# Reading the attention terms in natural query order on TensorE (moving operand with a stride of 32 words), with unstrided evictions on ScalarE

## The chip, the cores and the metric

The kernel runs on one core of a Trainium2 chip. A core has five engines that work side by side: TensorE (PE, matrix products, with a separate row PEld for loading its weights), VectorE (DVE), ScalarE (ACT), GpSimd (POOL) and SyncE (SP), which here issues all the transfers (DMAs). TensorE reads its operands from SBUF, the on-chip memory of 128 partitions, and writes its results to PSUM, from where ScalarE or VectorE fetch them ("evict" them) to SBUF. The metric is the device time of one execution in microseconds, as a median of several runs.

## The reference

There are 8 batches of 12 heads, 448 positions and 64 values per head. Attention with a soft cap comes first, and its result, with the heads side by side, goes through a gated block:

```
scores = cap * tanh(q @ k.T / 8 / cap)
attn   = exp(scores - max(scores))
attn   = attn / (sum(attn) + 1e-9)
x      = attn @ v                          # heads joined: 448 x 768
h      = relu(x @ w_in);  u, v = halves of h (512 each)
v_n    = (v - mean(v)) / sqrt(var(v) + 1e-6)
v_s    = w_spatial @ v_n + b_spatial
out    = (u * v_s) @ w_out
```

## The kernel before

The kernel has two bodies and a branch on the cap; with the cap of 30 the one for small caps runs (`pair_bnd`), in which no maximum has to be subtracted ahead of the exponential. Work on the attention goes by pairs of heads: 6 pairs in each of 8 batches, 48 in all. After the six pairs of a batch come the gated block's matrix products for that batch (`moe`), which are mixed on TensorE with the next batch's pairs.

The host hands over q with its 448 positions reordered. Position 14 i + b (i from 0 to 31, b from 0 to 13) stands in column 32 b + i. Everything up to the second product is in this order, "b outside, i inside", because VectorE's transposition of 32x32 blocks in the reduction needs the 32 positions of a block side by side.

The steps of one pair, with the names that the profile shows:

- One DMA brings q and k (`raw`). ScalarE makes the rounded copy `qh`, VectorE the remainder `ql`.
- TensorE forms the scores (L540) into `ps_s`, in two halves `j` of two blocks of 112 keys each, for both heads: keys on the partitions, queries along the free axis.
- ScalarE takes the tanh (L545) out of PSUM into `tp`, and then the exponential (L550) in place. `tp` is 112 partitions by 4 x 448 numbers: two key blocks by two heads. These are the terms of the softmax. There are two such tiles per pair.
- TensorE multiplies the terms with v (L559) into `ps_x`: the first head's result goes to PSUM partitions 0 to 63, the second's to 64 to 127. Four matmuls for each half, eight for a pair, accumulated over the four key blocks. There is one buffer of `ps_x`.
- ScalarE evicts `ps_x` to `xf` (L564). This copy also brings the positions back to natural order: it reads PSUM in order and writes SBUF with a stride of 14 words.
- The sums of the terms: for the first 10 pairs (`PE_SUMS`) TensorE forms them too, with a matrix of ones (L599) into a `ps_acc` buffer, eight matmuls into four groups of 32 PSUM partitions. ScalarE evicts them to `sx` (L602), again with the stride of 14 words. Four small DMAs bring four rows of `sx` to memory (`td`) and two more bring them back to `dt` with the positions across partitions. For the other 38 pairs VectorE does the sums, as it does the maxima for all of them (`red`, L580 to L587, then `st`, `md`, `dt`).
- VectorE forms the reciprocals in `dt`, DMAs bring them out (`rd`) and back, broadcast over the partitions (`rr`). GpSimd multiplies `xf` by `rr` (L645), and the result, split into a rounded part and a remainder (`xg`), is what the gated block reads.

The order of the work is made when the kernel is built. `Plan` simulates the engines with a duration for each task, and always starts the task with the lowest key among those whose inputs and buffers are there. The order that comes out is each engine's program. The durations are estimates written into the code: `act(S)` is 0.833 x 448 + 51 = 424 ns; the eviction of the second products has `act(S)`, that of the sums has 951 ns. TensorE's tasks of the second products and of the sums count 2 x 760 ns each.

Of the kernel before, what the change touches and what calls it, by code (L numbers as in the profile page):

```python
# [16 lines left out]
B, H, S, D = 8, 12, 448, 64  # L17
# [4 lines left out]
QB = 14  # L22
# [20 lines left out]
class Plan:  # L43
# [14 lines left out]
    def add(self, eng, dur, key, fn, deps=(), uses=(), allocs=(), lat=0.0, name="", mode="N"):  # L58
        t = Task()
        t.eng, t.dur, t.key, t.fn, t.lat, t.name, t.mode = eng, float(dur), key, fn, lat, name, mode  # L60
        t.lock = eng == "P" or eng == "V" and name not in self.OWN
        t.deps = [d for d in deps if d is not None]
        t.allocs = list(allocs)
        t.uses = list(dict.fromkeys(list(uses) + t.allocs))
        for u in t.uses:
            u.users += 1
        t.seq = len(self.tasks)
        self.tasks.append(t)
        return t
# [103 lines left out]
def act(n, extra=0):  # L173

    return 0.833 * n + 51 + 93 * extra


def act_s(n, extra=0):

    return 0.833 * n + 94 + 93 * extra  # L180
# [14 lines left out]
def gpc(n):  # L195
# [6 lines left out]
KB = S // 4  # L202
# [23 lines left out]
               ev=3.19, x=2.62, moe=0.79, span=12.63, step=0.24, mv=-1.51)  # L226
# [13 lines left out]
def attn_moe(ctx, tc, bounded, shared, qk, v, qk2, v2, cap, w_in, w_sp, w_out, out):  # L240
    nc = tc.nc
# [45 lines left out]
    if bounded:  # L287
# [4 lines left out]
        one = const.tile([128, 32], F32, name="one")  # L292
# [9 lines left out]
    add = plan.add  # L302
# [216 lines left out]
    def pair_bnd(b, hp, xf, rr):  # L519
# [3 lines left out]
        kk = lambda name, n=0: at + KEY[name] + KEY["step"] * n  # L523
# [7 lines left out]
        x, tps, exps, prev = Buf("x"), [], [], None  # L531
        for j in range(2):
            ps, tp = [Buf("s"), Buf("s")], Buf("tp")

            def scores(j=j, ps=ps):
                for i in range(2):
                    for n, (y, z) in enumerate(((qh, qh), (ql, qh), (qh, ql))):
                        for e in range(2):
                            r, c = slice(e * D, (e + 1) * D), S + (2 * j + i) * KB
                            nc.tensor.matmul(ps[i].t[:KB, e, :S], lhsT=y.t[r, c:c + KB], rhs=z.t[r, :S], start=(n == 0), stop=(n == 2))  # L540

            s = add("T", 6 * MM, kk("sc", j), scores, [t0, t2], [qh, ql, *ps], ps, name="sc", mode="R")
            for i in range(2):
                th = add("A", act(PW, 1), kk("th", j),
                         lambda i=i, ps=ps, tp=tp: nc.scalar.activation(  # L545
                             out=tp.t[:KB, i * PW:(i + 1) * PW].rearrange("p (e q) -> p e q", q=S), in_=ps[i].t[:KB, :, :S],
                             func=AF.Tanh, scale=ic[:KB]),
                         [s], [ps[i], tp], [tp] if i == 0 else [], name="tanh")
            ex = add("A", act_s(2 * PW, 1), kk("ex", j),
                     lambda tp=tp: nc.scalar.activation(out=tp.t[:KB], in_=tp.t[:KB], func=AF.Exp, scale=ca[:KB]), [th], [tp],  # L550
                     name="exp")
            tps.append(tp)
            exps.append(ex)

            def pv(j=j, tp=tp):
                for i in range(2):
                    for e in range(2):
                        c, o = 2 * j + i, (2 * i + e) * S
                        nc.tensor.matmul(x.t[e * D:(e + 1) * D, 0, :S], lhsT=vt.t[:KB, (2 * c + e) * D:(2 * c + e + 1) * D],  # L559
                                         rhs=tp.t[:KB, o:o + S], start=(c == 0), stop=(c == 3))  # L560

            prev = add("T", 2 * FF, kk("pv", j), pv, [ex, prev, t1], [vt, tp, x], [x] if j == 0 else [], name="pv", mode="C")

        z = add("A", act(S), kk("ev"), lambda: nc.scalar.copy(  # L564
            out=xf.t.rearrange("p (i b) -> p b i", b=QB), in_=x.t[:, 0, :S].rearrange("p (b i) -> p b i", i=32)), [prev], [x, xf],
            [xf], name="xev")

# [8 lines left out]
        for a, op, engs, key in ((0, ALU.max, E_RED, "mx"), (1, ALU.add, E_SUM, "sm"))[:1 if by_pe else 2]:  # L578
# [9 lines left out]
                out=st.t[:, 2 * a * QB:2 * (a + 1) * QB], in_=blk(r.t[:, PW:]), axis=AX.X), [d, *done], [r, st],  # L588
                [st] if a == 0 else [], name="red3"))
        row = lambda y: y.rearrange("(e p c) -> p e c", e=2, c=QB)  # L590
        sums = None
        if by_pe:
            acc, sx, td = Buf("acc"), Buf("sx"), Buf("td")

            def ones():
                for c in range(4):
                    for e in range(2):
                        o, i = e * D + c % 2 * 32, (c % 2 * 2 + e) * S
                        nc.tensor.matmul(acc.t[o:o + 32, 0, :S], lhsT=one[:KB], rhs=tps[c // 2].t[:KB, i:i + S], start=(c < 2), stop=(c > 1))  # L599

            sums = add("T", 2 * FF, kk("pv", 1) + 0.01, ones, exps, [u, w, acc], [acc], name="ones", mode="Q")
            sums = add("A", 951, kk("ev"), lambda: nc.scalar.copy(  # L602
                out=sx.t.rearrange("p (i b) -> p b i", b=QB), in_=acc.t[:, 0, :S].rearrange("p (b i) -> p b i", i=32)), [sums], [acc, sx],
                [sx], name="sev")
            sums = [add("S", HW, kk("dn"), lambda r=r: nc.sync.dma_start(out=td.t[r * S:(r + 1) * S], in_=sx.t[32 * r:32 * r + 1]), [sums],
                        [sx, td], [td] if r == 0 else [], lat=XL) for r in range(4)]
            two = lambda: dt.t[:32, 8 * QB:12 * QB].rearrange("p (e g c) -> p e g c", e=2, c=QB)
            sums = [add("S", HW, kk("dn"), lambda g=g: nc.sync.dma_start(
                out=two()[:, :, g], in_=td.t.rearrange("(e g p c) -> g p e c", e=2, g=2, c=QB)[g]), sums, [td, dt], [dt] if g == 0 else [],
                lat=XL) for g in range(2)]  # L610
# [6 lines left out]
            out=sec(0), in_=grp()[:, :, :2 * QB].rearrange("p g b -> p b g"), axis=AX.X), [d], [dt], name="mred2")  # L617
# [3 lines left out]
        else:  # L621
            d1 = add("V", 185, kk("dn"), lambda: nc.vector.reduce_sum(
                out=sec(1), in_=grp()[:, :, 2 * QB:].rearrange("p g b -> p b g"), axis=AX.X), [d0], [dt], name="sred2")
# [4 lines left out]
            out=row(rd.t), in_=sec(0).rearrange("p (e c) -> p e c", c=QB)), [d], [dt], [rd], lat=XL)  # L628
        out = [add("S", HH, kk("dn"), lambda e=e: nc.sync.dma_start(
            out=rr.t[e * D:(e + 1) * D], in_=rd.t[e * S:(e + 1) * S].unsqueeze(0).broadcast_to([D, S])), [d], [rd, rr],  # L630
            [rr] if e == 0 else [], lat=XF * D * S) for e in range(2)]
        return out + [z]

    def pair(b, hp):
        k = float(b * H + 2 * hp)
        xf, rr = Buf("xf"), Buf("rr")
        if bounded:
            deps = pair_bnd(b, hp, xf, rr)
        else:
            vt, vdep = v_any(b, hp, k - 1.2)  # L640
            after = []
            deps = [d for e in range(2) for d in head_any(b, 2 * hp + e, vt, vdep, xf, rr, after)]
        g = Buf("xg")
        k += KEY["x"] if bounded else 1.3
        m = add(E_X[0], st2(E_X[0], 448), k, lambda: eng[E_X[0]].tensor_tensor(xf.t, xf.t, rr.t, op=ALU.mult), deps, [xf, rr], name="xmul")  # L645
        c = add(E_X[1], ct(E_X[1], 448), k, lambda: copy(E_X[1], g.t[:, XH:], xf.t), [m], [xf], [g], name="xh")
        d = add(E_X[2], st2(E_X[2], 448), k, lambda: sub(E_X[2], g.t[:, :S], xf.t, f(g.t[:, XH:])), [c], [xf, g], name="xl")
        t = add(E_X[3], ct(E_X[3], D), k, lambda: copy(E_X[3], g.t[:, S:XH], xf.t[:, S - D:]), [m, c], [xf, g], name="xt")
        return g, [t, d]
# [222 lines left out]
```

## Time and profile before

| | |
|---|---|
| median of 3 runs | 802.78 us (802.62 to 805.45) |
| the profiled execution | 804.6 us |
| its span, first to last instruction | 802.7 us |
| mean granted TensorE clock | 0.99 |
| TensorE matmul records of the second products (L559) | 768, 157.2 us busy |
| TensorE matmul records of the sums (L599) | 160, 17.1 us busy |
| ScalarE copies of second products (L564) | 48, 46.2 us busy |
| ScalarE copies of sums (L602) | 10, 9.8 us busy |

The profile is one execution, taken by the hardware profiler. "Busy" is the time in which at least one instruction of a group ran on its engine. Matmuls overlap: a record's own duration includes the time in which it only finishes while the next is under way, so the busy time of a group is far below the count times the mean. A matmul on numbers of full precision leaves two records. The view of waits names for each idle stretch of an engine what ended it. The chain is the work that ended last, followed back from the end of the run.

### The profile page before, as it was taken

Reading aid. Unit: us, or ns where it says so; the run is one execution under the profiler, and the core shown is the slowest. Engines: PE = TensorE matmul, PEld = TensorE weight load, DVE = VectorE, ACT = ScalarE, POOL = GpSimd, SP = SyncE. Lnnn points to the kernel's source line nnn. Section 1 sums busy time; section 2 is a strip of 40 time slices with the busy share of each in tenths; the row PEclk is TensorE's granted clock in tenths of the full one; section 3 lists DMA queues with packets and bytes.
Section 4 is the critical chain, followed back from the end, with each engine's and each line's share of the span. In section 5 each row is a group of like instructions: output and inputs, shape, how many; then the busy total and the mean of one; then the engine's idle time right before and its main releaser. Section 6 shows DMA issues by size and latency. Waiting matters only on the chain.

```text
span 802.7 us, 11490 instructions
## 1 busy us (share of the span) xinstructions
PE 763.1 (95%) x4126; PEld 528.4 (66%) x4126; DVE 707.3 (88%) x934; ACT 575.5 (72%) x699; POOL 228.6 (28%) x179
## 2 busy tenths in 40 slices
PE   6878899979999999999999999999999999999997
PEld 2333456646776766667667677767677766767796
DVE  4979997899899997999999999999999999999340
ACT  4999877595777867687678876887677876874131
POOL 3131133341242103440143313330244212431150
PEclk8999999999999999999999999999999999999999
DMA  5544532433222332124221332223221332112102
GB/s 176 182 109 125 152 111 62 125 89 121 60 61 74 97 112 58 48 62 131 75 61 50 120 97 61 69 68 113 93 59 51 107 99 68 54 52 73 38 1 73
DMA packets 51254, 69.04 MB, mean 86 GB/s; under 512 B 23754, under 2 KB 36596, under 8 KB 51188
## 3 DMA queue, kind: packets, MB, share of 16 engines
q1 hardware_dynamic: 51188, 68.22, 28.7%
q8 instruction: 34, 0.56, 0.3%
q14 instruction: 32, 0.26, 0.1%
HBM read 55.70 MB, written 12.49 MB: 85 GB/s over the span
## 4 chain that ended last, share of the span: by engine, by line
PE 54%; DVE 24%; DMA 8%; ACT 7%; issue 5%; POOL 1%; SPq 1%; ACTq 0%; DVEq 0%; POOLq 0%
PE ps_x L559 10%; DVE red L580 10%; PE ps_s L540 9%; PE ps_acc L678 4%; PE ps_acc L679 4%; PE ps_acc L680 4%; DVE red L585 3%; DVE st L587 3%; ACT tp L545 2%; DMA dt<-md 2%; PE ps_acc L772 2%; ACT tp L550 2%; PE ps_acc L774 2%; PE ps_acc L773 2%; PE ps_acc L794 2%
## 5 line engine op out<-in xcount | busy, mean ns | idle before, releaser
L545 ACT ACTIVATE tp<-ps_s,capt 112x896 f32<-112x896 f32 x192 | 184.6, 1005 | 9.9 <-PE ps_s L540 8.9
L580 DVE TENSOR_TENSOR red<-tp 112x1792 f32<-112x1792 f32 x86 | 180.6, 2110 | 10.0 <-ACT tp L550 10.0
L550 ACT ACTIVATE tp<-tp,capt 112x1792 f32<-112x1792 f32 x96 | 172.4, 1796 | 2.3
L645 POOL TENSOR_TENSOR xf<-xf,rr 128x448 f32<-128x448 f32 x48 | 86.2, 1797 | 280.1 <-DMA rr<-rd 267.6
L559 PE MATMUL ps_x<-tp,v 112*64 112x448 f32 x768 | 157.2, 549 | 4.6 <-ACT tp L550 2.7
L559 PEld LDWEIGHTS ps_x<-tp,v 112*64 112x64 f32 x768 | 50.4, 137 | 87.2 <-issue 75.7
L580 DVE TENSOR_TENSOR red<-red 112x896 f32<-112x896 f32 x86 | 103.4, 1203 | 0.5
L585 DVE STREAM_TRANSPOSE red<-red 128x896 f32<-128x896 f32 x86 | 94.0, 1093 | 0.9
L587 DVE TENSOR_REDUCE st<-red 128x28 f32<-128x896 f32 x86 | 90.8, 1077 | 1.1
L540 PE MATMUL ps_s<-qh 64*112 64x448 f32 x384 | 81.2, 417 | 10.2 <-ACT tp L545 6.4
L540 PE MATMUL ps_s<-qh,ql 64*112 64x448 f32 x384 | 72.8, 372 | 6.6 <-DVE ql L306 6.5
L306 POOL TENSOR_TENSOR xg<-o,xg 128x448 fp32r<-128x448 f32 x32 | 46.1, 1443 | 107.4 <-ACT xg L310 107.4
L540 PEld LDWEIGHTS ps_s<-qh 64*112 64x112 f32 x384 | 34.0, 173 | 63.8 <-issue 28.1
L540 PE MATMUL ps_s<-ql,qh 64*112 64x448 f32 x384 | 72.2, 368 | 0.0
L678 PE MATMUL ps_acc<-xg,wi_h 128*128 128x448 f32 x186 | 69.7, 375 | 1.3 <-ACT xg L310 1.2
L794 PE MATMUL ps_acc<-xg,wo_h 128*128 128x448 f32 x184 | 69.3, 376 | 1.5 <-DVE o L779 1.2
L679 PE MATMUL ps_acc<-xg,wi_h 128*128 128x448 f32 x186 | 68.9, 371 | 1.1 <-DVE xg L306 1.1
L795 PE MATMUL ps_acc<-xg,wo_h 128*128 128x448 f32 x184 | 67.4, 366 | 1.6 <-POOL xg L306 1.6
L680 PE MATMUL ps_acc<-xg,wi_l 128*128 128x448 f32 x186 | 68.6, 369 | 0.0
L796 PE MATMUL ps_acc<-xg,wo_l 128*128 128x448 f32 x184 | 67.4, 366 | 0.0
L310 ACT CAST xg<-xf 128x448 fp32r<-128x448 f32 x96 | 36.5, 402 | 34.3 <-POOL xf L645 31.7
L306 DVE TENSOR_TENSOR ql<-raw,qh 128x896 fp32r<-128x896 f32 x48 | 53.3, 1111 | 7.2 <-ACT qh L310 7.2
(123 smaller groups left out, 1386.7 us busy)
## 6 DMA issues: line engine op xcount, KB each, us to landing
raw<-in_qk SPq DMA_DIRECT2D x48, 448.0 KB
v<-in_v SPq DMA_DIRECT2D x48, 224.0 KB
rr<-rd SPq DMA_DIRECT2D x96, 112.0 KB
out<-o SPq DMA_DIRECT2D x48, 224.0 KB
w<-in_w_in SPq DMA_DIRECT2D x12, 512.0 KB
xg<-in_w_out SPq DMA_DIRECT2D x12, 256.0 KB
md<-st SPq DMA_DIRECT2D x38, 28.0 KB
dt<-md SPq DMA_DIRECT2D x38, 28.0 KB
```

What stands on the lines that cost most here:

```text
L306: eng[e].tensor_tensor(o, a, b, op=ALU.subtract)
L540: nc.tensor.matmul(ps[i].t[:KB, e, :S], lhsT=y.t[r, c:c + KB], rhs=z.t[r, :S], start=(n == 0), stop=(n == 2))
L545: lambda i=i, ps=ps, tp=tp: nc.scalar.activation(out=tp.t[:KB, i * PW:(i + 1) * PW].rearrange("p (e q) -> p e q", q=S), in_=ps[i].t[:KB, : ...
L550: lambda tp=tp: nc.scalar.activation(out=tp.t[:KB], in_=tp.t[:KB], func=AF.Exp, scale=ca[:KB]), [th], [tp],
L559: nc.tensor.matmul(x.t[e * D:(e + 1) * D, 0, :S], lhsT=vt.t[:KB, (2 * c + e) * D:(2 * c + e + 1) * D], rhs=tp.t[:KB, o:o + S], start=(c == ...
L580: tt = lambda g, o_, i0, i1, op=op: eng[g].tensor_tensor(o_, i0, i1, op=op)
L585: d = add("V", dve(PW), kk(key), lambda r=r: nc.vector.transpose(out=blk(r.t[:, PW:]), in_=blk(r.t[:, :PW])), [d], [r], name="vtr")
L587: done.append(add("V", dve(PW), kk(key), lambda r=r, a=a, red=red: red(out=st.t[:, 2 * a * QB:2 * (a + 1) * QB], in_=blk(r.t[:, PW:]), axi ...
L645: m = add(E_X[0], st2(E_X[0], 448), k, lambda: eng[E_X[0]].tensor_tensor(xf.t, xf.t, rr.t, op=ALU.mult), deps, [xf, rr], name="xmul")
L678: nc.tensor.matmul(ps, lhsT=wi_h[:, c, fs], rhs=x[:, XH:], start=(c == 0), stop=False)
L679: nc.tensor.matmul(ps, lhsT=wi_h[:, c, fs], rhs=x[:, :S], start=False, stop=False)
L680: nc.tensor.matmul(ps, lhsT=wi_l[:, c, fs], rhs=x[:, XH:], start=False, stop=(c == NP - 1))
```

## The change

The reordering moves from ScalarE's writes to TensorE's reads. A helper `nat` gives a view of 448 columns in the order "i outside, b inside": 32 runs of 14 numbers that lie 32 words apart. The second products and the sums read `tp` through it as their moving operand, so that PSUM holds the natural order. The two evictions become plain copies of 448 columns. The planner's duration for the eviction of the sums goes from 951 to `act(S)`; that of the second products had `act(S)` before.

```diff
+            nat = lambda y: y.rearrange("p (b i) -> p i b", i=32)
+
             def pv(j=j, tp=tp):
...
-                                         rhs=tp.t[:KB, o:o + S], start=(c == 0), stop=(c == 3))
+                                         rhs=nat(tp.t[:KB, o:o + S]), start=(c == 0), stop=(c == 3))
...
-        z = add("A", act(S), kk("ev"), lambda: nc.scalar.copy(
-            out=xf.t.rearrange("p (i b) -> p b i", b=QB), in_=x.t[:, 0, :S].rearrange("p (b i) -> p b i", i=32)), [prev], [x, xf],
-            [xf], name="xev")
+        z = add("A", act(S), kk("ev"), lambda: nc.scalar.copy(out=xf.t, in_=x.t[:, 0, :S]), [prev], [x, xf], [xf], name="xev")
...
-                        nc.tensor.matmul(acc.t[o:o + 32, 0, :S], lhsT=one[:KB], rhs=tps[c // 2].t[:KB, i:i + S], start=(c < 2), stop=(c > 1))
+                        nc.tensor.matmul(acc.t[o:o + 32, 0, :S], lhsT=one[:KB], rhs=nat(tps[c // 2].t[:KB, i:i + S]), start=(c < 2), stop=(c > 1))
...
-            sums = add("A", 951, kk("ev"), lambda: nc.scalar.copy(
-                out=sx.t.rearrange("p (i b) -> p b i", b=QB), in_=acc.t[:, 0, :S].rearrange("p (b i) -> p b i", i=32)), [sums], [acc, sx],
-                [sx], name="sev")
+            sums = add("A", act(S), kk("ev"), lambda: nc.scalar.copy(out=sx.t, in_=acc.t[:, 0, :S]), [sums], [acc, sx], [sx], name="sev")
```

The diff takes two lines away, so line numbers behind the second products differ: the eviction of L564 is L566 in the changed kernel, L559 is L561, and lines from L603 on are two lower.

Since a duration in the plan changes, every engine's order changes too. On ScalarE the first difference stands right behind the first two evictions. The rows below are ScalarE's program in the fill, from the exponential of the second pair's first half (`tp_285`) on; `wi_h` is a cast of weights for the gated block, and a number behind a name tells its buffers apart. Before:

```order
L550 ACTIVATE tp_285<-tp_285,capt_58 112x1792
L564 COPY xf_323<-ps_x_248 128x14x32
L602 COPY sx_326<-ps_acc_295 128x14x32
L310 CAST qh_336<-raw_262 128x896
L545 ACTIVATE tp_342<-ps_s_309,capt_58 112x896
L545 ACTIVATE tp_342<-ps_s_310,capt_58 112x896
L310 CAST wi_h_167<-wy_223 128x512
L550 ACTIVATE tp_342<-tp_342,capt_58 112x1792
```

And in the changed kernel, from the same exponential on:

```order
L550 ACTIVATE tp_285<-tp_285,capt_58 112x1792
L566 COPY xf_323<-ps_x_248 128x448
L602 COPY sx_326<-ps_acc_295 128x448
L310 CAST wi_h_167<-wy_223 128x512
L310 CAST qh_339<-raw_262 128x896
L545 ACTIVATE tp_343<-ps_s_309,capt_58 112x896
L545 ACTIVATE tp_343<-ps_s_310,capt_58 112x896
L550 ACTIVATE tp_343<-tp_343,capt_58 112x1792
```

The two copies stay where they are and lose their stride; the cast of weights from `wy_223` moves ahead of the next pair's `qh`, which stood right behind the copies.

On TensorE the program is the same, but for the reading of `tp`, up to the fourth pair. There the sets of second products (`ps_x`) and of sums (`ps_acc`, with `one`) of that pair stand in this order before, with score products (`ps_s`) of the next pair between them; x4 is four matmuls of one half:

```order
L559 MATMUL ps_x_581<-tp_478,v_402 64x448 x4
L559 MATMUL ps_x_581<-tp_542,v_402 64x448 x4
L540 MATMUL ps_s_605<-qh_535 112x448 x2
L540 MATMUL ps_s_605<-qh_535,ql_546 112x448 x2
L540 MATMUL ps_s_605<-ql_546,qh_535 112x448 x2
L540 MATMUL ps_s_606<-qh_535 112x448 x2
L540 MATMUL ps_s_606<-qh_535,ql_546 112x448 x2
L540 MATMUL ps_s_606<-ql_546,qh_535 112x448 x2
L599 MATMUL ps_acc_623<-tp_478,one_177 32x448 x4
L599 MATMUL ps_acc_623<-tp_542,one_177 32x448 x4
```

In the changed kernel the same place reads:

```order
L599 MATMUL ps_acc_586<-tp_481,one_177 32x448 x4
L599 MATMUL ps_acc_586<-tp_542,one_177 32x448 x4
L540 MATMUL ps_s_600<-qh_535 112x448 x2
L540 MATMUL ps_s_600<-qh_535,ql_545 112x448 x2
L540 MATMUL ps_s_600<-ql_545,qh_535 112x448 x2
L540 MATMUL ps_s_601<-qh_535 112x448 x2
L540 MATMUL ps_s_601<-qh_535,ql_545 112x448 x2
L540 MATMUL ps_s_601<-ql_545,qh_535 112x448 x2
L561 MATMUL ps_x_621<-tp_481,v_402 64x448 x4
L561 MATMUL ps_x_621<-tp_542,v_402 64x448 x4
```

The sums now stand ahead of the scores and the second products behind them. The number of matmuls and their output shapes are as before.

## The prediction

> **What bounds the kernel now.** I read the page's busy table first, then its slices, then the chain.
>
> ```profile
> span 802.7 us, 11490 instructions
> PE 763.1 (95%) x4126; PEld 528.4 (66%) x4126; DVE 707.3 (88%) x934; ACT 575.5 (72%) x699; POOL 228.6 (28%) x179
> PE   6878899979999999999999999999999999999997
> ACT  4999877595777867687678876887677876874131
> PE 54%; DVE 24%; DMA 8%; ACT 7%; issue 5%; POOL 1%; SPq 1%; ACTq 0%; DVEq 0%; POOLq 0%
> ```
>
> TensorE (PE) is busy 95% of the span and carries 54% of the chain. The slices split the run in two: a fill of about eight slices (20 us each) in which PE has holes, and the rest, in which it has almost none. The view of busy time by stretches gives sizes (first column the stretch, then its length, then busy time of PE, PEld, DVE, ACT, POOL).
>
> ```profile
> 20.00:40.00 20.00, 16.63 (x116) 6.92 (x116) 18.16 (x25) 20.00 (x21) 2.44 (x3) 1.00 0.58 184
> 40.00:60.00 20.00, 15.64 (x102) 6.37 (x100) 15.52 (x21) 18.83 (x21) 7.63 (x8) 0.91 0.44 110
> 60.00:80.00 20.00, 16.22 (x114) 7.21 (x114) 19.58 (x26) 19.10 (x23) 3.14 (x3) 1.00 0.43 125
> 80.00:100.00 20.00, 16.96 (x97) 9.10 (x99) 19.97 (x33) 17.86 (x20) 2.96 (x2) 1.00 0.53 148
> 400.00:500.00 100.00, 99.70 (x549) 70.62 (x548) 97.61 (x127) 75.75 (x90) 31.37 (x23) 1.00 0.27 78
> ```
>
> From 20 to 100 us PE works 65.45 of 80 us, while ScalarE (ACT) works 75.79: the fill is paced by ACT and what hangs on it, with VectorE close. Later PE works 99.70 of 100 us and ACT 75.75: there ACT time is covered by PE, and any PE time is paid in full. So the two halves of this change are priced in different stages: ACT's saving in the fill, TensorE's reading over the whole run.
>
> **Part 1, ScalarE.** The groups by shape (last numbers before the bar: busy us, mean ns of one):
>
> ```profile
> L564 ACT COPY xf<-ps_x 128x448 f32<-128x448 f32 x48 | 46.2, 962 | 8.1 <-DVE xg L306 5.8 <-PE ps_x L559 1.2 <-PE ps_acc L703 0.7
> L602 ACT COPY sx<-ps_acc 128x448 f32<-128x448 f32 x10 | 9.8, 981 | 3.9 <-PE ps_acc L599 3.9
> L310 ACT COPY o<-ps_acc 128x448 f32<-128x448 f32 x46 | 24.4, 535 | 45.7 <-DMA out<-o 24.3 <-PE ps_acc L796 18.0 <-PE ps_s L540 1.8
> ```
>
> L310 copies the same 128x448 out of PSUM without a stride: 535 ns. So the new copies should take 535: 48 x (962 - 535) = 20.5 us, 10 x (981 - 535) = 4.5 us, 25.0 us of ACT in all. How much of it lies on the path? The chain for 20 to 80 us, summed by line, says:
>
> ```profile
> by line: issue 14.2%; ACT tp L545 13.7%; ACT tp L550 13.3%; DMA dt<-md 13.0%; DVE red L580 12.1%; ACT xf L564 4.5%; ACT sx L602 4.0%; DVE ql L306 3.6%; ACT qh L310 3.5%; DVE dt L619 2.9%; SPq L608 2.6%; ACT wi_h L310 2.1%; DMA td<-sx 2.1%;
> POOL xf L645 <- DMA rr<-rd: 267.6, 35, 16.9
> PEld ps_x L559 <- ACT xf L564: 4.3, 6, 1.8
> PE ps_x L559 <- ACT xf L564: 1.8, 2, 1.4
> ```
>
> The two copies hold 8.5% of 60 us, 5.1 us; shortened by 44% (427 of 962) that is 2.3 us. Between 80 us and the last sums near 154 us I add 1 us. The last two rows are TensorE waiting for xf, since there is one ps_x buffer: 6.1 us at most, of which 44% is 2.7 us; part is in the 2.3 already, so I count 1.7. **Sum: -5 us.** The floor is 0, if the chain steps to VectorE or the maxima's DMA (13.0%) at once; the most is about -9, all the relief of some 20 copies in the first 100 us. The xf <-rr row (267.6 us) shows why more isn't possible: the multiply that reads xf waits for the reciprocals' DMA, not for this copy, so that is late next.
>
> **Part 2, TensorE.** No instruction is added: each matmul still is one instruction of 448 columns with the same output, only its moving operand is read 32 words apart, in runs of 14. No row of this trace has such a matmul, so I bound it. First what a step costs now (start, length, then the operation and count):
>
> ```profile
> 304.09 1.72 PE L559 MATMUL ps_x<-tp,v 112*64 112x448 f32 x8
> 65.69 3.23 PE L559 MATMUL ps_x<-tp,v 112*64 112x448 f32 x16
> 72.92 1.71 PE L599 MATMUL ps_acc<-tp,one 112*32 112x448 f32 x16
> L559 PE MATMUL ps_x<-tp,v 112*64 112x448 f32 x768 | 157.2, 549 | 4.6 <-ACT tp L550 2.7 <-ACT xf L564 1.8
> L599 PE MATMUL ps_acc<-tp,one 112*32 112x448 f32 x160 | 17.1, 545 | 0.0
> ```
>
> The program has 384 second products; the trace has 768 records, two for each. They run two side by side (the two heads), so eight records are four steps: (3.23 - 1.72) / 4 = 0.378 us a step, 0.843 ns a column. The sums run four side by side and 16 records take 1.71 us, so also four steps: four streams from the same partitions cost no more than two. In all 768 / 2 + 160 / 4 = 424 steps; **each 1 ns on a step is 0.42 us of the run.**
>
> Now the two ends. How fast can TensorE fetch 4-byte elements? The products with xg (rounded, one record each), 12 matmuls apart, and ScalarE's own pace:
>
> ```profile
> 299.64 0.39 PE L705 MATMUL ps_acc<-wi_h,xg 128*128 128x512 f32 x1
> 302.36 0.39 PE L705 MATMUL ps_acc<-wi_h,xg 128*128 128x512 f32 x1
> L545 ACT ACTIVATE tp<-ps_s,capt 112x896 f32<-112x896 f32 x192 | 184.6, 1005 | 9.9 <-PE ps_s L540 8.9 <-DVE xg L379 0.7
> L550 ACT ACTIVATE tp<-tp,capt 112x1792 f32<-112x1792 f32 x96 | 172.4, 1796 | 2.3
> ```
>
> 2.72 us / 12 / 512 = 0.443 ns a column there, so the steps of tp use 0.843 / 0.443 = 1.90 fetch slots a column. ScalarE's slot is (1796 - 1005) / 896 = 0.883 ns an element, and its strided copy adds 427 / 448 = 0.953 ns: a strided element costs it two slots of its own (a write, in that row). Carried over in slots, a strided column on TensorE costs 2 x 0.443 = 0.886 ns where it has 0.843 now: between nothing and (0.886 - 0.843) x 448 x 424 = +8 us. That holds if each element is fetched once and kept for both slots. Carried over in ns, or if both slots are fetches, the column doubles or worse: +0.378 x 424 = +160 us, or +0.953 x 448 x 424 = +181 us. Below zero is excluded: nothing here is read less often. **I take 0,** by the slot reading, because the fetch pace of the xg rows, TensorE's own, is nearer to the case than another engine's write; the ends 0 and +181 stay for the range.
>
> The Trainium skill speaks against this edit: "SBUF — State Buffer", section "Door 1: The DMA port swizzle", says that an access which crosses to a new 16-byte line pays a penalty and that two hits a line are needed to absorb the latency; here every element is on a line of its own. It gives no time: read in slots it leaves the sum at -5, read in ns it makes it +160 or more. The strided ScalarE copy (962 against 535 ns) agrees that there is a penalty; no run so far shows it on TensorE.
>
> **Part 3, the order.** The planner now costs a sums copy at 424 instead of 951 and so moves work on every engine. In the fill a product set and a sums set trade places, and ACT's weight casts move by a step. After 200 us PE has about 11 idle us of 603, the tail included, so there is little to win; a bad turn costs a wait like these:
>
> ```profile
> PE ps_s L540 <- DVE ql L306: 6.5, 6, 2.2
> PE ps_s L540 <- ACT qh L310: 3.7, 1, 3.7
> ```
>
> One such wait more or less is 2.2 to 3.7 us: I cost the order at 0, with +-4.
>
> **Sum.** The profiled execution took 804.6 us: -5 + 0 + 0 gives 799.6. The median of the runs is 1.8 lower, so 798 us, with a range of its own from 790 to 811 (-9 and -4; +8 and +4, rounded).
>
> **Rivals.**
> *A, TensorE pays for the stride* (slower). Both slots of a column are fetches from a line not at hand: steps go from 0.378 to 0.756 us. For it: ScalarE's doubled copy, the two records per product. Against: the 1.90 slots in hand, and four streams at no extra cost. The place is the whole run, at 99.70% PE without cover; in the fill the holes (80 - 65.45 us) take some 10, ACT's relief 4: 802.8 + 160 - 14 = 949. It decides early: 5 us / 424 = 12 ns a step eats the gain, 21 ns makes it slower by over 0.5%.
>
> *B, a small penalty.* VectorE's strided reads:
>
> ```profile
> L580 DVE TENSOR_TENSOR red<-tp 112x1792 f32<-112x1792 f32 x86 | 180.6, 2110 | 10.0 <-ACT tp L550 10.0
> L580 DVE TENSOR_TENSOR red<-red 112x896 f32<-112x896 f32 x86 | 103.4, 1203 | 0.5
> L587 DVE TENSOR_REDUCE st<-red 128x28 f32<-128x896 f32 x86 | 90.8, 1077 | 1.1
> L616 DVE TENSOR_REDUCE dt<-dt 32x28 f32<-32x112 f32 x48 | 16.0, 334 | 8.4 <-DMA dt<-md 8.2
> ```
>
> (2110 - 1203) / 896 = 1.01 ns an element; L587 then has 170 ns fixed, and L616, which reads with a stride, has 334 - 170 - 113 = 51 ns left over 112 elements, 0.45 ns each. On TensorE: 0.45 x 448 x 424 = +85, so 802.8 + 85 - 14 = 874.
>
> *C, both at once*: two fetches of ScalarE's 1.84 ns each in place of 0.843: + 2.83 x 448 x 424 = +538, about 1330.
>
> *D, nothing but the order*: ACT's relief is covered, time 799 to 807.
>
> **How the numbers follow.** Forecast with D 0.54; A 0.30, B 0.07, C 0.09. Half a percent, 4 us, is about what a measurement of this kernel can tell from no change. The forecast's -5 with +-4 from the order splits into 0.34 faster, 0.17 within, 0.03 slower. With A to C slower: 0.49. The range runs from 790 to 985 (A with ScalarE's 181 and little cover: 802.8 + 181, rounded up); it leaves out C and some ends, under 2 in 10. The sign is open; the likeliest single case is the small gain.
>
> **What would show it.** Right: sets of eight strided records still take 1.72 us and 16 sums 1.71, the two copies read 535 ns, PE's idle time from 20 to 100 us shrinks below 14.55 us. Wrong: records of the products far over 549 ns with no wait ahead of them (A, B, C by size); or unchanged records and copies still near 962 ns, which would mean that PSUM's reading and not the write's stride made them slow; or unchanged records, short copies, and new waits on qh, ql or md.

## The result, and the profile after

| | before | changed | ratio, 95% interval |
|---|---|---|---|
| median | 803.62 us (802.62 to 805.45, 4 runs) | 955.37 us (955.11 to 955.77, 4 runs) | 1.187 [1.184, 1.190] |
| span of the profiled execution | 802.7 us | 953.4 us | |

The change makes the kernel 18.7% slower. The forecast of 798 us failed; the time is near that of rival A (949). The page of the changed kernel, with the rows that answer to those shown of before: the busy table, the slices of TensorE (PE) and ScalarE (ACT), and the chain by engine.

```profile
span 953.4 us, 11513 instructions
PE 929.7 (98%) x4126; PEld 537.3 (56%) x4126; DVE 715.8 (75%) x934; ACT 560.6 (59%) x699; POOL 226.3 (24%) x179
PE   7989999998999999999999999999999999999997
ACT  5777655555565666565666656567566665656131
PE 92%; DVE 3%; ACT 3%; DMA 1%; issue 1%; POOL 0%; SPq 0%; ACTq 0%; DVEq 0%
```

TensorE holds 92% of the chain, where it had 54%: the holes of the fill have all but closed (from 20 to 100 us TensorE now works 76.73 of 80 us, where it worked 65.45), and little else sets the pace. PE's busy time rose by 166.6 us (929.7 - 763.1), and its idle time shrank from 39.6 to 23.7 us; the difference, 150.7 us, is what the span grew by. The groups by shape name the matmuls, and the timeline (start, length, operation, count) shows a set:

```profile
L561 PE MATMUL ps_x<-tp,v 112*64 112x448 f32 x768 | 309.4, 958 | 3.2 <-ACT xf L566 2.0 <-ACT tp L550 1.2
L599 PE MATMUL ps_acc<-tp,one 112*32 112x448 f32 x160 | 39.5, 1095 | 0.7 <-ACT stg L718 0.7
L566 ACT COPY xf<-ps_x 128x448 f32<-128x448 f32 x48 | 25.6, 533 | 79.4 <-PE ps_x L561 71.0 <-issue 6.4 <-DVE xg L306 1.9
```

```profile
61.68 4.19 PE L599 MATMUL ps_acc<-tp,one 112*32 112x448 f32 x16
67.22 6.50 PE L561 MATMUL ps_x<-tp,v 112*64 112x448 f32 x16
```

Sixteen records of the second products take 6.50 us where they took 3.23, and sixteen of the sums 4.19 where they took 1.71. Over the run the products grew by 152.2 us and the sums by 22.4, 174.6 together; TensorE's whole busy time rose by 8 us less, since groups overlap and the others differ by some microseconds. ScalarE's copy is as short as forecast, 533 ns, but look at the end of its row: it now waits 71.0 us for the products. A faster copy is of no use to an engine that waits for the one made slower.

### The profile page after: what moved, and what is told of

Read it like the earlier page. It is cut to its first block, busy times and chain, and to the rows that moved or that the text cites. A ratio compares the mean times of both kernels' runs of the same rounds, so it can differ in the third digit from the quotient of the medians.

```text
span 953.4 us, 11513 instructions
## 1 busy us (share of the span) xinstructions
PE 929.7 (98%) x4126; PEld 537.3 (56%) x4126; DVE 715.8 (75%) x934; ACT 560.6 (59%) x699; POOL 226.3 (24%) x179
## 4 chain that ended last, share of the span: by engine, by line
PE 92%; DVE 3%; ACT 3%; DMA 1%; issue 1%; POOL 0%; SPq 0%; ACTq 0%; DVEq 0%
PE ps_x L561 31%; PE ps_s L540 13%; PE ps_acc L676 4%; PE ps_acc L792 4%; PE ps_acc L677 4%; PE ps_acc L678 4%; PE ps_acc L794 4%; PE ps_acc L793 4%; PE ps_acc L599 4%; PE ps_acc L701 3%; PE ps_acc L702 3%; PE ps_acc L703 3%; PE ps_acc L770 2%; PE ps_acc L771 2%; PE ps_acc L772 2%; PE ps_acc L698 1%
## 5 line engine op out<-in xcount | busy, mean ns | idle before, releaser
L561 PE MATMUL ps_x<-tp,v 112*64 112x448 f32 x768 | 309.4, 958 | 3.2 <-ACT xf L566 2.0
L580 DVE TENSOR_TENSOR red<-tp 112x1792 f32<-112x1792 f32 x86 | 176.7, 2063 | 23.3 <-ACT tp L550 23.3
L561 PEld LDWEIGHTS ps_x<-tp,v 112*64 112x64 f32 x768 | 56.7, 150 | 191.6 <-issue 180.4
L643 POOL TENSOR_TENSOR xf<-xf,rr 128x448 f32<-128x448 f32 x48 | 76.7, 1599 | 359.9 <-DMA rr<-rd 344.5
L580 DVE TENSOR_TENSOR red<-red 112x896 f32<-112x896 f32 x86 | 109.4, 1272 | 0.5
L310 ACT CAST qh<-raw 128x896 fp32r<-128x896 f32 x48 | 45.3, 945 | 69.9 <-PE ps_s L540 69.1
L306 POOL TENSOR_TENSOR xg<-o,xg 128x448 fp32r<-128x448 f32 x32 | 50.5, 1583 | 132.8 <-ACT xg L310 128.4
L566 ACT COPY xf<-ps_x 128x448 f32<-128x448 f32 x48 | 25.6, 533 | 79.4 <-PE ps_x L561 71.0
```

What stands on the lines that cost most here:

```text
L306: eng[e].tensor_tensor(o, a, b, op=ALU.subtract)
L580: tt = lambda g, o_, i0, i1, op=op: eng[g].tensor_tensor(o_, i0, i1, op=op)
```

## The experiments

Each edit is against the kernel before unless it says otherwise. Some of these kernels leave the positions in another order or place; the expectation says which. The four kernels in which the step differs by pair or by column block ran once each; what is read from them are single records, sets and the steps of a chain, not their time.

### ScalarE's half alone, in the new order and in the old

Unstrided copies, terms read in order. The first kernel has the changed planner duration too (the second edit below), the other the old one:

```diff
-            out=xf.t.rearrange("p (i b) -> p b i", b=QB), in_=x.t[:, 0, :S].rearrange("p (b i) -> p b i", i=32)), ...
+            out=xf.t, in_=x.t[:, 0, :S]), ...
...
-            sums = add("A", 951, kk("ev"), ...
+            sums = add("A", act(S), kk("ev"), ...
```

> ScalarE's half of the change alone, with the changed kernel's planner durations and so its order; TensorE reads the terms without a stride, so the positions come out in the wrong order. Theory (all of the loss is TensorE's strided reading, and ScalarE's relief is worth the 5 us of the prediction): both copies take about 535 ns, records of second products stay at 549 ns and their busy time at 157 us, the time is 795 to 803 us. Rival (the new order of the work is a good part of the loss): records as before, but the time is above 815 us.

> The same as the run before it, but with the planner's old 951 ns for the sums copy, so in the old order; the positions come out in the wrong order. Theory: copies 535 ns, 795 to 803 us, within 4 us of the kernel with the new order. Rival (the order matters): over 8 us away from that kernel.

| kernel | median | ratio to before, 95% interval |
|---|---|---|
| short copies, new order | 810.26 us | 1.008 [1.005, 1.011] |
| short copies, old order | 800.05 us | 0.994 [0.992, 0.996] |

In the old order, the short copies are worth 0.6% of 804.39 us, 4.7 us (3.1 to 6.2): the prediction's term of 5. In the new order the same copies end 0.8% above the kernel before. So the order alone costs 10 to 11 us (10.2 between the medians, 1.4% between the ratios), where I had written 0 with +-4. That is not the main loss, since the products did not change here, but it was no noise either. The products' rows, new order first:

```profile
L559 PE MATMUL ps_x<-tp,v 112*64 112x448 f32 x768 | 158.6, 554 | 4.8 <-ACT xf L564 2.6
L559 PE MATMUL ps_x<-tp,v 112*64 112x448 f32 x768 | 158.0, 551 | 1.8 <-ACT tp L550 1.8
```

The view of busy time by stretches shows the place; the first two rows are the new order, the last two the old:

```profile
20.00:200.00 180.00, 154.48 (x880) 86.44 (x877) 162.17 (x243) 135.30 (x173) 58.85 (x48) 0.95 0.40 116
200.00:700.00 500.00, 495.17 (x2678) 355.03 (x2679) 475.99 (x591) 363.27 (x449) 137.58 (x99) 1.00 0.26 78
```

```profile
20.00:200.00 180.00, 161.39 (x928) 92.87 (x929) 165.97 (x252) 139.98 (x179) 51.21 (x48) 0.96 0.41 120
200.00:700.00 500.00, 497.69 (x2698) 357.97 (x2695) 481.39 (x595) 369.87 (x454) 142.19 (x101) 1.00 0.27 79
```

The first number behind the length is PE's busy time: 154.48 of 180 us in the fill against 161.39, so 6.9 us of the loss are there, and 2.5 us in the 500 us behind. TensorE's waits for 100 to 200 us in the new order are many small ones for different engines, the longest these:

```profile
PE ps_acc L675 <- DVE xg L306: 2.2, 1, 2.2
PE ps_x L559 <- ACT xf L564: 2.0, 1, 2.0
PE ps_acc L790 <- ACT xg L310: 1.8, 1, 1.8
```

The granted clock may be a part of the loss. Over the run it was 0.977 to 0.983 in the new order and 0.982 to 0.990 in the old, about 0.005 apart; that is some 4 us of 800 if TensorE is the bound throughout (an estimate, and an upper one). In the profile of the new order a set of sums at 52.87 us ran at a clock of 0.50 and took 3.21 us, where 1.71 is usual. Which of the moved tasks brings the waits, and whether the lower clock follows from them, wasn't tried. A sums copy that in truth takes 541 ns was closer to the plan's 424 than to its 951, and still the plan with 951 gave the better order: a truer duration did not make a better plan.

### TensorE's half alone, and the changed kernel in the old order

The first kernel reads the terms with the stride and keeps the strided copies and the old order. The second is the changed kernel with the old duration in the plan (the second diff is against the changed kernel); beside it ran the changed kernel once more.

```diff
-                                         rhs=tp.t[:KB, o:o + S], start=(c == 0), stop=(c == 3))
+                                         rhs=nat(tp.t[:KB, o:o + S]), start=(c == 0), stop=(c == 3))
...
-                        nc.tensor.matmul(acc.t[o:o + 32, 0, :S], lhsT=one[:KB], rhs=tps[c // 2].t[:KB, i:i + S], ...
+                        nc.tensor.matmul(acc.t[o:o + 32, 0, :S], lhsT=one[:KB], rhs=nat(tps[c // 2].t[:KB, i:i + S]), ...
```

```diff
-            sums = add("A", act(S), kk("ev"), ...
+            sums = add("A", 951, kk("ev"), ...
```

> TensorE's half of the change alone: strided reading of the terms for the products and the sums, the old strided copies and the old order; the positions are reordered twice and come out wrong. Theory: the products' busy time is again about 309 us and the sums' 39 us, and the time is 955 to 970 us: the changed kernel's 955 plus what ScalarE's relief was worth, at most 9 us. Rival (the order or the short copies made the products wait): the time falls well below 950 us.

> The changed kernel with the old 951 ns of the sums copy in the plan, so in the old order; strided reading and short copies as in the changed kernel, the output is the reference's. Theory (with unstrided reading the new order cost about 10 us; under the strided products TensorE covers part of it): 945 to 952 us, 4 to 10 us below the changed kernel. Rival (the new order costs nothing once TensorE is the bound throughout): within 3 us of the changed kernel.

> The changed kernel itself, beside the run before it on the same chip. Expected 953 to 958 us, as before, by both theories.

| kernel | median | ratio to before, 95% interval |
|---|---|---|
| strided reading only, old order | 950.03 us | 1.181 [1.177, 1.186] |
| changed kernel, old order | 949.87 us | 1.180 [1.176, 1.183] |
| changed kernel again | 955.65 us | 1.187 [1.184, 1.190] |

The row of the products in the first of these kernels:

```profile
L561 PE MATMUL ps_x<-tp,v 112*64 112x448 f32 x768 | 310.2, 959 | 3.3 <-ACT xf L566 2.2
```

Its products are busy for as long as in the changed kernel (309.4), and its sums too (39.4 against 39.5). The strided reading alone brings 950 us, below the 955 to 970 expected: I had counted on the copies' 5 to 9 us on top, and had not counted on the order. Between the first two kernels stand the short copies. The two medians, from two chips, differ by 0.2 us, which is less than the intervals can tell: with TensorE as the bound, the 25 us that ScalarE saves bring nothing that shows. Between the last two, on one chip, stands the order, 5.8 us, about half of what it cost when TensorE had holes. Here too the granted clock differs, 0.994 to 0.996 in the old order and 0.985 to 0.994 in the new.

### What a stride costs on TensorE, by its size

Only the second products change: each of a batch's six pairs reads `tp` in its own way, on a line of its own.

```diff
+                        if hp == 0:
+                            nc.tensor.matmul(xo, lhsT=lh, rhs=y, **kw)
+                        elif hp == 1:
+                            nc.tensor.matmul(xo, lhsT=lh, rhs=nat(y, 2), **kw)
+                        elif hp == 2:
+                            nc.tensor.matmul(xo, lhsT=lh, rhs=tp.t[:KB, e * S:e * S + 3 * S - 2:3], **kw)
+                        elif hp == 3:
+                            nc.tensor.matmul(xo, lhsT=lh, rhs=nat(y, 4), **kw)
...
```

> Only the second products are changed, and each of a batch's six pairs reads the terms in its own way, on its own line: in order, with a step of 2, 3, 4, 8 and 32 words (positions or terms come out wrong for the last five). Two streams side by side, as in the kernel. Theory 1 (an element of a new 16-byte line costs two fetch slots, and full precision fetches each element twice): steps of 0.378 us for 1 and for 2 words, about double for 4, 8 and 32 alike, something between for 3. Theory 2 (a price that grows with the distance): 4, 8 and 32 words differ by over 10% in a step. Theory 3 (any step other than 1 breaks the stream): 2 words cost as much as 32.

The view of one line gives the shortest, median and longest record. Lines 564 to 574 are in order, then steps of 2, 3, 4, 8 and 32 words:

```profile
L564 PE MATMUL ps_x<-tp,v x128: 539/539/1009, 16.5 to 725.4; 112*64 112x448 f32 x128
L566 PE MATMUL ps_x<-tp,v x128: 553/555/609, 26.6 to 744.0; 112*64 112x448 f32 x128
L568 PE MATMUL ps_x<-tp,v x128: 759/761/796, 37.0 to 760.9; 112*64 112x448 f32 x128
L570 PE MATMUL ps_x<-tp,v x128: 965/967/982, 51.6 to 780.1; 112*64 112x448 f32 x128
L572 PE MATMUL ps_x<-tp,v x128: 982/983/997, 67.3 to 794.1; 112*64 112x448 f32 x128
L574 PE MATMUL ps_x<-tp,v x128: 930/945/1032, 79.1 to 811.8; 112*64 112x448 f32 x128
```

Read the medians against 539. Two words are all but free (+16 ns), three cost half (+222), four cost all (+428), and 8 and 32 cost no more (+444, +406). A step was 378 ns, so the full price is slightly more than a doubling. The price begins between steps of 8 and 16 bytes and does not grow with the distance from there on; the short runs of 14 play no part, since the step of 4 has runs of 112. The Trainium skill's line of 16 bytes and its two hits ("SBUF — State Buffer", section "Door 1: The DMA port swizzle") agree with these rows in where the price begins. With a step of 3 words two of four elements share such a line and two stand alone, and half the price is paid. The rounded operands further below do not agree: there 2 words, two hits on a line, already cost the full price.

### One stream, two, and four

First the second products with one stream at a time: both heads go to the same half of PSUM for pairs 0 to 2 of a batch (lines 564 to 568: in order, 4 words, 32 words); pairs 3 to 5 have two streams with 16, 64 and 32 words.

```diff
+                        if hp == 0:
+                            nc.tensor.matmul(x.t[c // 2 * D:(c // 2 + 1) * D, 0, :S], lhsT=lh, rhs=y, **kw)
+                        elif hp == 1:
+                            nc.tensor.matmul(x.t[c // 2 * D:(c // 2 + 1) * D, 0, :S], lhsT=lh, rhs=nat(y, 4), **kw)
...
```

> Second products again, by pair of a batch: pairs 0 to 2 write both heads' products to the same half of PSUM's partitions, so that only one stream runs at a time (in order, step of 4 words, step of 32 words); pairs 3 to 5 have two streams side by side with steps of 16, 64 and 32 words. Products come out in wrong places. Theory 1 (the price is one of each stream): one stream in order 0.378 us a matmul record, one strided stream 0.75 to 0.78, the same as two side by side; 16, 32 and 64 words alike. Theory 2 (streams share one way of reading, and the price comes from sharing): one strided stream stays near 0.378 us a record, and two together 0.77.

```profile
L564 PE MATMUL ps_x<-tp,v x128: 538/539/592, 16.6 to 817.3; 112*64 112x448 f32 x128
L566 PE MATMUL ps_x<-tp,v x128: 964/966/981, 27.9 to 841.8; 112*64 112x448 f32 x128
L568 PE MATMUL ps_x<-tp,v x128: 930/942/1000, 45.2 to 863.4; 112*64 112x448 f32 x128
L570 PE MATMUL ps_x<-tp,v x128: 926/928/1000, 65.9 to 882.4; 112*64 112x448 f32 x128
```

A lone strided stream has records of 966 and 942 ns, the same as two side by side (967 and 945 above), and its eight records take 6.49 and 6.23 us where eight in order take 3.22. Two streams with 16, 64 and 32 words have medians of 928, 942 and 947 ns. So the price is each stream's own; sharing is not the cause. Then the sums, four streams side by side, with steps by pair:

```diff
-                        nc.tensor.matmul(acc.t[o:o + 32, 0, :S], lhsT=one[:KB], rhs=tps[c // 2].t[:KB, i:i + S], ...
+                        if hp == 0:
+                            nc.tensor.matmul(ao, lhsT=one[:KB], rhs=y, **kw)
+                        elif hp == 1:
+                            nc.tensor.matmul(ao, lhsT=one[:KB], rhs=nat(y, 2), **kw)
...
```

> Second products in order; only the sums of the first 10 pairs, four streams side by side, read with steps: pairs of a batch 0 to 5 in order, 2, 4, 32, 8 and 16 words, each on its own line; sums come out wrong. If four streams pay as two do: records of 539, 555, 967, 945, 983 and 928 ns as in the runs on the second products. If streams share one limit on new 16-byte lines: the steps of 4 words and more take clearly longer than with two streams (over 1050 ns), the step of 2 words too, since two streams' worth of new lines are asked for with four.

The timeline's sets of 16 records; lines 603, 605, 607, 609, 611, 613 are in order, 2, 4, 32, 8 and 16 words:

```profile
25.23 1.73 PE L603 MATMUL ps_acc<-tp,one 112*32 112x448 f32 x16
35.06 1.78 PE L605 MATMUL ps_acc<-tp,one 112*32 112x448 f32 x16
45.05 3.34 PE L607 MATMUL ps_acc<-tp,one 112*32 112x448 f32 x16
59.66 3.88 PE L609 MATMUL ps_acc<-tp,one 112*32 112x448 f32 x16
64.87 3.40 PE L611 MATMUL ps_acc<-tp,one 112*32 112x448 f32 x16
75.02 3.27 PE L613 MATMUL ps_acc<-tp,one 112*32 112x448 f32 x16
```

Four streams with 4, 8 or 16 words take 3.27 to 3.40 us for their four steps, like two streams for theirs (6.50 and 6.62 us for eight, with 4 and 8 words). Of the steps tried only 32 words, the change's own, take longer: 3.88 here and 4.18 in a second set, with a median record of 1074 ns, and 3.78 to 4.19 in the ten sets of the changed kernel. Something is shared, but it shows only at this distance, and it is small: the sums' 22.4 us are 7 more than the 15.1 of a plain doubling (40 steps of 0.378 us). What is shared wasn't found.

### The same stride on rounded operands

Is the price a fixed time for each fetch, or a number of TensorE's slots that full precision pays twice because it fetches each element twice? The products that form u have rounded operands, one record each. Their moving operand is read with steps of 1, 2, 4 and 32 words for the four column blocks.

```diff
+                        if j == 0:
+                            nc.tensor.matmul(ps, lhsT=l, rhs=y(r, 1), start=st, stop=sp)
+                        elif j == 1:
+                            nc.tensor.matmul(ps, lhsT=l, rhs=y(r, 2), start=st, stop=sp)
...
```

> The terms are read in order again; instead the products that form u (rounded operands, one record each, one stream of 448 columns) read their moving operand in order, with steps of 2, 4 and 32 words for the four column blocks j, each on its own line; positions come out wrong. In order a record follows the last after 0.203 us. Theory 1 (two slots for each fetch; the products at full precision doubled because they fetch each element twice): 0.40 us for 4 and 32 words, 0.20 for 2. Theory 2 (one fetch per element at a fixed price of some 1.7 ns, whatever the pace): 0.75 us for 4 and 32 words. Theory 3 (only full precision pays): 0.20 us for all.

The timeline, first and last row with `wi_l` of a chain for each step (lines 682, 684, 686, 688); the last starts 15 records after the first:

```profile
330.25 0.36 PE L682 MATMUL ps_acc<-xg,wi_l 128*128 128x448 f32 x1
333.29 0.36 PE L682 MATMUL ps_acc<-xg,wi_l 128*128 128x448 f32 x1
336.29 0.58 PE L684 MATMUL ps_acc<-xg,wi_l 128*128 128x448 f32 x1
342.22 0.58 PE L684 MATMUL ps_acc<-xg,wi_l 128*128 128x448 f32 x1
351.82 0.58 PE L686 MATMUL ps_acc<-xg,wi_l 128*128 128x448 f32 x1
357.87 0.58 PE L686 MATMUL ps_acc<-xg,wi_l 128*128 128x448 f32 x1
361.26 0.56 PE L688 MATMUL ps_acc<-xg,wi_l 128*128 128x448 f32 x1
366.99 0.56 PE L688 MATMUL ps_acc<-xg,wi_l 128*128 128x448 f32 x1
```

Divided by 15: 0.203 us a record in order, 0.395 at 2 words, 0.403 at 4, 0.382 at 32. For 4 and 32 words that is theory 1: a strided column is 0.85 to 0.90 ns, about two of TensorE's own slots of 0.443 to 0.453. A price of 1.7 ns for each fetch, whatever the pace, would have given 0.75, and is out. Full precision pays +0.41 to +0.43 us on a record where a rounded one pays +0.18 to +0.20, twice as much, as if each element were fetched twice. No record shows the two fetches themselves, and one row speaks against so simple a picture: 2 words double the rounded record, which no theory had, and are free at full precision. That stays open. It does not touch the loss, which is at 32 words.

Two slots are a count at the full clock only. In the second run of the changed kernel eight strided records of the products, at 16.53 us, ran at a granted clock of 0.50 throughout and took 3.47 us; five such sets at 1.00 take 3.27 to 3.36. In the kernel with the short copies and the new order sixteen records of the products in order, at 170.35 us, ran almost wholly at 0.50 and took 5.82 us, where 3.23 is usual. The lower clock nearly doubles the time of reading in order and leaves that of reading with the stride almost as it was. What sets the pace of the strided reading is not the granted clock; what it is stays open.

### Two ways that leave TensorE's reading alone

The reordering can also be done where PSUM is read, or where it is written. In the first kernel ScalarE reads PSUM with a stride of 32 words and writes SBUF in order; in the second TensorE writes its results with a stride of 14 words and ScalarE copies without one. Both read the terms in order and keep the old order of work.

```diff
-            out=xf.t.rearrange("p (i b) -> p b i", b=QB), in_=x.t[:, 0, :S].rearrange("p (b i) -> p b i", i=32)), ...
+            out=xf.t.rearrange("p (i b) -> p i b", b=QB), in_=x.t[:, 0, :S].rearrange("p (b i) -> p i b", i=32)), ...
```

```diff
+            spread = lambda y: y.rearrange("p (i b) -> p b i", b=QB)
...
-                        nc.tensor.matmul(x.t[e * D:(e + 1) * D, 0, :S], lhsT=...
+                        nc.tensor.matmul(spread(x.t[e * D:(e + 1) * D, 0, :S]), lhsT=...
```

> No strided reading of SBUF by TensorE: ScalarE's two copies read PSUM with a stride of 32 words and write SBUF in order, old planner durations. The output is the reference's. If the cost of the old copies is that of writing with a stride, and reading PSUM with one is free: copies near 535 ns, time 795 to 803 us, as with the copies that have no stride. If a stride costs ScalarE two slots wherever it is: copies near 960 ns, time 801 to 806 us, no different from before.

> TensorE reads the terms in order and writes its results with a stride of 14 words into PSUM, so that they lie there in natural order; ScalarE's copies have no stride; old planner durations. The output is the reference's. If TensorE's writing with a stride is free: products' busy time 157 us, copies 535 ns, 795 to 803 us. If it pays as its strided reading did: products near 309 us, 950 to 960 us.

| kernel | median | ratio to before, 95% interval |
|---|---|---|
| ScalarE reads PSUM strided | 798.7 us | 0.994 [0.992, 0.996] |
| TensorE writes PSUM strided | 798.32 us | 0.993 [0.990, 0.995] |

The rows by shape, of the first kernel and then of the second:

```profile
L564 ACT COPY xf<-ps_x 128x448 f32<-128x448 f32 x48 | 25.3, 528 | 5.7 <-DVE xg L306 5.2
L559 PE MATMUL ps_x<-tp,v 112*64 112x448 f32 x768 | 159.6, 555 | 4.6 <-ACT tp L550 3.6 <-ACT xf L564 1.0
```

```profile
L566 ACT COPY xf<-ps_x 128x448 f32<-128x448 f32 x48 | 25.3, 528 | 6.6 <-DVE xg L306 4.1 <-PE ps_x L561 1.1 <-PE ps_s L540 1.0
L561 PE MATMUL ps_x<-tp,v 112*64 112x448 f32 x768 | 157.8, 550 | 3.2 <-ACT tp L550 2.1 <-ACT xf L566 1.0
```

A strided read of PSUM costs ScalarE nothing (528 ns, with or without), and neither does a strided write cost TensorE (550 ns a record, 549 before). The old copies' 962 ns were the price of writing SBUF with a stride. Both kernels gain what the change was forecast to gain (5.7 and 6.0 us against the kernel before beside them), and both beat the kernel before and the changed one.

## Why the prediction was wrong, point by point

- **Part 1, the copies: right.** 533 ns instead of 535, and 4.7 us (3.1 to 6.2) where 5 was written. The condition was right too, in the other direction: worth something while ScalarE paces the fill, and nothing that shows once TensorE covers it.
- **Part 2, the step that failed:** "I take 0, by the slot reading". The term put at 0 measured 152.2 us for the products and 22.4 for the sums; the step of 0.378 us grows by 0.41 to 0.44. The size of a fetch was right at the full clock: on rounded operands a strided column costs about two of TensorE's own slots, and not ScalarE's time. What failed is that the 1.90 slots a column in the rows of before would cover it; they were no spare time. The likeliest reason is that the condition "each element is fetched once and kept for both slots" does not hold, since at full precision a strided record pays twice what a rounded one pays; no run shows the fetches. The rows of before could not tell the two apart, and I took the xg rows for a sign of room. They show a pace for reading in order, and that is not a price for reading out of order. The measured time lies in the range of 790 to 985 only because the range was drawn to hold rival A.
- **Rival A: right in what is paid, and in size with some luck.** Its 160 us came out as 152.2 for the products (written 145.2) and 22.4 for the sums (written 15.1). Its 949 us is within 0.1% of the changed kernel in the old order, but there TensorE's busy time grew by 166.9 us (to 930.0) and 21.6 us of its idle time closed, where 160 and 14 were written: two misses that cancel. The rest, 5.8 us, is the order, which it had at nothing. The argument against it, four streams at no extra cost, was beside the point: the price is each stream's own.
- **Rivals B and C: wrong in size.** They add 0.45 and 2.83 ns to a column. At full precision the strided column costs 0.91 to 0.99 ns more (406 to 444 ns over 448 columns). B's figure is that of rounded operands (0.40 to 0.45 ns), which these products do not have.
- **Part 3, the order: wrong in size.** Written as 0 with +-4; it costs 10 to 11 us with unstrided reading and 5.8 us in the changed kernel, the lower granted clock included. The reason given, that PE had little idle time to win, bounds the gain and not the loss. Rival D, with 799 to 807 us for the relief gone and only the order left, is topped by the 810.26 us of the short copies in the new order.
- **The inner range:** with the relief at its floor of 0 and both +8 and +4 its upper end is 802.8 + 12 = 815 us, and not 811. Nothing that was measured turns on it.

## What to carry to other kernels

A stride has its price at one port and not at another, and it has to be looked up or measured for the port in question: here it nearly doubled ScalarE's writes to SBUF and a little more than doubled TensorE's reads from it, and was free where ScalarE read PSUM with 32 words and where TensorE wrote it with 14. Moving a cost from an engine with idle time to the one that is the bound needs a measured price first; a spare-looking pace of the bound engine in another kind of instruction is none. And where a planner makes the order, a changed duration is a change of its own and should be measured apart from the edit.

## What the runs showed that was not expected

- On rounded operands a step of 2 words already doubles a matmul (0.203 to 0.395 us), while at full precision it costs 16 of 539 ns.
- Four streams with a step of 32 words take 3.78 to 4.19 us for 16 records, where 4, 8 and 16 words take 3.27 to 3.40.
- TensorE writes 448 results with a stride of 14 words into PSUM as fast as in order, in records of 550 ns.
- A granted clock of 0.50 takes products in order from 3.23 to 5.82 us for 16 records, and leaves strided ones almost as they were (3.47 us for eight, against 3.27 to 3.36).
